# Joint transposes of q and k, an earlier x of pair 1, and four idle products in a fused attention and spectral-mix kernel

## The chip, the cores and the metric

The kernel runs on one core of one Trainium2 chip. A core has TensorE (matrix products into PSUM), VectorE, ScalarE and GpSimd, a queue engine (SyncE, called SP in the profile) and 16 DMA engines. The metric is the device time of one execution in microseconds (us); the median of several executions is compared.

## The reference

What is computed, cut to what matters:

```python
def _attn_ref(q, k, v, s):                       # q, k, v: (8, 8, 576, 64); s: (8, 8, 576)
    scores = np.matmul(q, k.transpose(0, 1, 3, 2)) / np.sqrt(64)
    cum = np.cumsum(np.maximum(s, 0.0), axis=-1)
    bias = -(cum[:, :, :, None] - cum[:, :, None, :])
    scores = np.where(causal, -1e9, scores + np.minimum(bias, 0.0))
    return np.matmul(softmax(scores), v)

def _moe_ref(x, w_r, w_i, w_ch):                 # x: (8, 576, 512); w_r, w_i: (64, 512, 512)
    X = np.fft.rfft(x, axis=1)                   # only the first 64 modes are mixed
    Yr = einsum('bmd,mde->bme', Xr, w_r) - einsum('bmd,mde->bme', Xi, w_i)
    Yi = einsum('bmd,mde->bme', Xr, w_i) + einsum('bmd,mde->bme', Xi, w_r)
    u = x + np.fft.irfft(Y, n=576, axis=1)
    return u + np.maximum(u @ w_ch, 0.0)
```

The heads of the attention's output, laid side by side, are the x of the second part.

## The kernel before

**Attention.** The loop over `n` (line 564) runs 32 times; each turn, called a sequence here, does two heads of one batch entry: group `g` of four (two heads each, 128 columns of x), batch entry `b`. A q/k tile (`loads_qk`, line 148) holds two sequences: q of both heads stands in partitions 0 to 63 and k in 64 to 127, each partition with 18 rows of 64 values. `transposes` (line 332) turns it into `qt` and `kt`, which have the 64 head values in the partitions: 36 products of 64x64 on TensorE in two halves of 18, q into PSUM partitions 0 to 63 and k into 64 to 127 of the tile `tr_ps`, which has one buffer; then four copies out of PSUM: q and k of the first half and q of the second on VectorE, k of the second on ScalarE (line 344). The transposes of sequence n + 1 are made in turn n, the halves around `scores(n, 1)`. `scores` (line 366) makes score products and their exponentials on ScalarE (line 390), `av` (line 401) the product with v and the division by the sum (VectorE, `den`, `rcp`, `x_all`), `fft` (line 435) the forward transform of x into `xs`.

**Modes.** For each group the 64 modes are mixed in eight chunks of eight modes (`modes`, line 455): 16 products of 32 columns with weights that stream in from DRAM, summed over the groups in `y_acc`. Chunks of the first three groups are put among the sequences (`mode_steps`, line 239); those of the last group come after attention. A chunk has four quarters of weights: real and imaginary, and for each four of its eight modes. All weight, q, k and v loads are issued by GpSimd's queue in the order of the program (line 234), each once the place that it fills is free.

**x times w_ch.** The output is cut into 18 pairs of 128-token tiles. For a pair, `x_transposed` (line 629) transposes x and VectorE casts it out of PSUM, and `x_times_wch` (line 644) multiplies it with w_ch. Pairs 0 and 1 keep this product open in PSUM until y is known; pair 1 consists of half tiles. In the last sequences (`first_pairs`, line 512) and among the last group's chunks (`work`, line 718) other pairs' products are made ahead.

**The end.** After the last group's chunks 0 to 5 (line 833) follow chunk six (line 852) and chunk seven (line 868). `y_transposed` transposes a chunk's result and ScalarE copies it, `y_times_wch` multiplies it with w_ch and VectorE casts that to `v_sb`, which SP spreads into `yv` (`spread`, line 496); `gather` (line 688) does this in bulk for earlier chunks. In chunk seven the products of pairs 0 and 1 that need no last chunk (`first_u`, `first_z`) are put ahead of the third and the last quarter. `auxpool` has two PSUM buffers that `yp`, `yt_ps`, `v_ps` and others take in turn. The string of steps at line 924 finishes all pairs.

Each engine runs its instructions in program order, so where a step is written decides what it stands behind.

Of the kernel before, what the change touches and what calls it, by code (L numbers as in the profile page):

```python
# [9 lines left out]
FP32 = mybir.dt.float32  # L10
FP16 = mybir.dt.float16
BF16 = mybir.dt.bfloat16
# [6 lines left out]
def kernel(  # L19
# [11 lines left out]
    nc = tc.nc  # L31
    B, H, S, D = q.shape
    NM = moe_w_r.shape[0]
    DM = H * D
# [16 lines left out]
    NF = NT - 1  # L51
    RP = P // 4
    R = S // RP
    RH = R // 2
    W = 2 * P
    NWN = S // W
    NK = 2 * NWN
# [271 lines left out]
        for h in range(2):  # L329
            nc.sync.dma_start(out=qt[n % NQ][D : D + 1, h, :], in_=ncum_sb[p0 + h : p0 + h + 1, :])  # L330

    def transposes(n, half):
        if n >= N:
            return
        src = loaded[n][:, n % 2, :].rearrange("p (r d) -> p r d", d=D)[:, half * RH : half * RH + RH]
        ps = trpool.tile([P, RH, 2 * RP], BF16, name="tr_ps", tag="tr")
        for r in range(RH):
            for i in range(2):
                rows = slice(HP * i, HP * i + HP)
                nc.tensor.transpose(ps[rows, r, :], src[rows, r, :], ident16[rows, rows])  # L340
        for i, dst in enumerate((qt, kt)):
            copy = (nc.vector.tensor_copy, nc.scalar.copy)[half * i]
            to = dst[n % NQ][:D].rearrange("d h (p r) -> d h p r", r=R)
            copy(  # L344
                out=to[:, :, :, half * RH : half * RH + RH],
                in_=ps[HP * i : HP * i + HP].rearrange("d r (h p) -> d h p r", h=2),
            )

    def scores4(n, ps):
# [51 lines left out]
    def av(n, h):  # L401
        if n < 0:
            return
        g, b = divmod(n, B)
        pt = p_sb[(2 * n + h) % NP_]
        ps = avpool.tile([P, NT, VW], FP32, name="av_ps", tag="av")
        todo = []
        for I in range(NT):
            t0 = first_token(b, I)
            for x in range(2 * min((t0 + P - 1) // W + 1, NWN)):  # L410
                w, r = divmod(x, 2)
                o = poff[x] + t0 - w * W
                todo.append((I, r, pt[:, o : o + P], v2[n % NV][:, bass.ds((2 * w + h) * W + P - 1 + NCH * r, NCH)]))
        rows = slice(NL * h, NL * h + NL)
        todo.append((NT - 1 - b % 2, 1, p4[n % 2][rows, :], v4[g % 2][rows, b, :NCH]))

        for i, (I, r, lhsT, rhs) in enumerate(todo):
            nc.tensor.matmul(  # L418
                ps[:, I, r : r + NCH], lhsT, rhs, start=(i == 0), stop=(i == len(todo) - 1),
                skip_group_check=True,  # L420
            )
        den = rpool.tile([P, NT], FP32, name="den", tag="den")
        nc.vector.tensor_reduce(  # L423
            out=den, in_=ps[:, :, 0 : VW : NCH], axis=mybir.AxisListType.X, op=ALU.add
        )
        rcp = rpool.tile([P, NT], FP32, name="rcp", tag="rcp")
        nc.vector.reciprocal(out=rcp, in_=den)
        nc.vector.tensor_tensor(  # L428
            out=x_all[:, g, b, :, D * h : D * h + D],
            in0=ps[:, :, 1 : NCH],  # L430
            in1=rcp.unsqueeze(2).to_broadcast([P, NT, D]),
            op=ALU.mult,
        )

    def fft(n):
        if n < 0:
            return
        g, b = divmod(n, B)
        ps = auxpool.tile([P, 2, 3 * HM], FP32, name="ft_ps", tag="aux")
        for T in range(NT):  # L440
            nT = tails[T]
            for q_ in range(2):
                nc.tensor.matmul(  # L443
                    ps[HP * q_ : HP * q_ + HP].rearrange("p h f -> p (h f)"),
                    x_all[:nT, g, b, T, q_::2], Ff_sb[:nT, T, :],
                    start=(T == 0), stop=(T == NT - 1),
                    tile_position=(0, HP * q_), skip_group_check=True,
                )
        for h in range(2):
            for q_ in range(2):  # L450
                a = ps[HP * q_ : HP * q_ + HP, h, : 2 * HM].rearrange("p (r m) -> p r m", r=2)
                a = bass.AP(tensor=a.tensor, offset=a.offset, ap=[a.ap[0], [HM, 2]] + list(a.ap[1:]))
                nc.vector.tensor_copy(out=xs[g % 2][HP * h : HP * h + HP, q_, :, h, :, b, :], in_=a)  # L453
# [102 lines left out]
    with tc.tile_pool(name="sc_psum", bufs=2, space=PSUM) as scpool, \  # L556
            tc.tile_pool(name="tr_psum", bufs=1, space=PSUM) as trpool, \
            tc.tile_pool(name="av_psum", bufs=1, space=PSUM) as avpool:
        cum_rows(0)
        transposes(0, 0)  # L560
        transposes(0, 1)
        load(loads_qk(2) + loads_v(2))
        pad_p()
        for n in range(N):
            if n in (0, 2):
                nc.vector.memset(xs_flat[n // 2].bitcast(FP32), 0.0)
            tails_due = loads_tails(n // B + 1)[n % B - 3 : n % B - 2] if 2 < n % B < 5 else []
            load((loads_qk(n + LA) if n % 2 else []) + loads_v(n + LA) + tails_due, loads_w(on_chip[n]))
            cum_rows(n + 1)
            scores(n, 0)  # L570
            av(n - 1, 1)
            if n % B:
                mode_products(n)
            transposes(n + 1, 0)
            scores(n, 1)
            i = first_pairs[n - N + len(first_pairs)] if n >= N - len(first_pairs) else None
            if i is not None:
                first_transposed(i, 0)
            transposes(n + 1, 1)
            fft(n - 1)  # L580
            av(n, 0)
            if i is not None:
                first_product(i, 0)
                first_transposed(i, 1)
            if n % B == 0:
                mode_products(n)
            if i is not None:
                first_product(i, 1)
            if n == N // 2:
                nc.gpsimd.dma_start(out=wch_sb, in_=moe_w_ch.rearrange("(dt p) e -> p dt e", p=P))  # L590
        av(N - 1, 1)
        fft(N - 1)
# [36 lines left out]
    def x_transposed(i):  # L629
        xts[i] = xt_sb[len(xts) % 2]  # L630
        for x, (b, T) in enumerate(pairs[i]):
            ps = upool.tile([P, DT, P], FP32, name="xt_ps", tag="u")
            for rows, bb, ident in parts(b, T):
                for dt in range(DT):
                    nc.tensor.matmul(
                        ps[:, dt, rows], x_all[: rows.stop - rows.start, dt, bb, T, :],
                        ident, start=True, stop=True, skip_group_check=True,
                    )
            nc.vector.tensor_copy(out=xts[i][:, x], in_=ps)  # L639
# [4 lines left out]
    def x_times_wch(i, last):  # L644
        for x in range(2):
            start_z(i, x)
            for dt in range(DT):
                nc.tensor.matmul(  # L648
                    zs[i, x], xts[i][:, x, dt, :], wch_sb[:, dt, :],
                    start=(dt == 0), stop=(last and dt == DT - 1), skip_group_check=True,  # L650
                )
# [25 lines left out]
    def y_times_wch(c, yt):  # L677
        vp = auxpool.tile([P, DM], FP32, name="v_ps", tag="aux")
        for dt in range(DT):
            nc.tensor.matmul(  # L680
                vp, yt[:, dt, :], wch_sb[:, dt, :], start=(dt == 0), stop=(dt == DT - 1)
            )
        vb = spool.tile([P, DM], FP16, name="v_sb", tag="v")
        nc.vector.tensor_copy(out=vb, in_=vp)
        spread(c, 1, vb)
        return vb
# [146 lines left out]
    for c in range(NCK - 2):  # L833
        yb = modes(NG - 1, c)
        for x in range(TAKE[c] - 1):
            work()
        if c == NCK - 3:
            x_transposed(0)
        yt = y_transposed(yb, c)
        if TAKE[c]:  # L840
            work()
        if c >= NY:
            if c == NCK - 3:
                x_times_wch(0, False)
            y_times_wch(c, yt)
            if c == NCK - 3:
                gather(NY, NCK - 2, (), (0,))
        elif c == NY - 1:
            gather(0, NY, (1, 3), (1, 0))
    assert not order_z and not ahead  # L850
    c = NCK - 2
    yb6 = modes(NG - 1, c)
    x_transposed(1)
    yt = y_transposed(yb6)
    x_times_wch(1, False)
    vb6 = y_times_wch(c, yt)


    def first_u():
        add_x(0)  # L860
        add_y(u_of(0), 0, 0, slice(0, GK))
        add_last(u_of(0), 0, yb6, c=0)

    def first_z(i):
        add_y(z_of(i), i, 1, slice(0, GK))
        add_last(z_of(i), i, vb6, c=0)

    yb = modes(NG - 1, NCK - 1, {2: lambda: (first_u(), first_z(0)), 3: lambda: first_z(1)})

    yt = spool.tile([P, DT, P], FP16, name="yt_sb", tag="yt")  # L870
    for x in range(2):
# [95 lines left out]
```

The softmax here doesn't subtract the row's maximum and nothing guards it: scores larger than these inputs give would overflow.

## Time and profile before

| What | Value |
|---|---|
| median of 6 runs | 444.13 us (443.84 to 445.58) |
| profiled execution, its own time | 445.08 us |
| its span, first to last instruction | 443.0 us |
| mean granted TensorE clock | 0.923 |
| TensorE busy | 341.1 us (77%) |
| VectorE busy | 253.0 us (57%) |
| ScalarE busy | 226.1 us (51%) |
| GpSimd busy | 246.1 us (56%) |
| moved by DMA | 93.25 MB, mean 210 GB/s |
| chain that ended last | DMA 61%, PE 18%, DVE 9% of the span |

How to read it: the page cuts the span into 40 equal slices and gives each engine's busy share in each; "PEclk" is the TensorE clock that was granted, in tenths of full speed. "The chain of waits" follows the last instruction back, at each step to what released it; a line has its start, its length in us, its engine, tile and kernel line, and the number of instructions. In the timeline a line has the start, the busy time, the engine, the kernel line, the operation, what is written from what, and the shape; in brackets the idle time before it and what ended it. In a table of stretches, a row has the stretch, its length, and for TensorE, its weight loads, VectorE, ScalarE and GpSimd the busy time and the number of instructions; then the granted clock, the DMA share and GB/s. Engines: PE is TensorE, DVE VectorE, ACT ScalarE, POOL GpSimd. An engine's idle time costs nothing unless something on the path to the end waits for it.

### The profile page before, as it was taken

The numbers are of one execution on the slowest core, as the hardware profiler recorded it, in microseconds if no ns is written. First come the engines' busy times: TensorE is split into PE (matmuls) and PEld (weight loads), VectorE is DVE, ScalarE is ACT, GpSimd is POOL, SyncE is SP. The second block draws the span as 40 slices with busy tenths as digits, with TensorE's granted clock in tenths as the row PEclk, the third lists the DMA queues.
The fourth block names the chain that finished last, engine by engine and source line by source line (L and its number), as shares of the span: only waits on it lengthen the run. The fifth ranks groups of instructions, "written<-read, shape, count | busy, mean of one in ns | idle before, by whom it ended". The sixth has DMA issues, their size and how long they took to land.

```text
span 443.0 us, 10830 instructions
## 1 busy us (share of the span) xinstructions
PE 341.1 (77%) x4411; PEld 206.6 (47%) x4411; DVE 253.0 (57%) x574; ACT 226.1 (51%) x421; POOL 246.1 (56%) x385
## 2 busy tenths in 40 slices
PE   0788988988676996593946928898987987749994
PEld 0455655655454653361634505555653445324441
DVE  7766776666545664462633605767655454432696
ACT  1476787367544643472543604665650544320794
POOL 7765665565565656365655546465644444440495
PEclk9998999999969798988895968999997999988998
DMA  9999999999999999999999999999999999997498
GB/s 175 201 206 206 204 206 205 207 206 206 209 194 205 205 208 206 209 206 208 204 206 205 209 208 198 206 205 206 192 208 211 209 210 210 210 217 155 145 388 344
DMA packets 72768, 93.25 MB, mean 210 GB/s; under 512 B 29760, under 2 KB 31296, under 8 KB 72720
## 3 DMA queue, kind: packets, MB, share of 16 engines
q0 software_dynamic: 63408, 81.29, 104.8%
q1 hardware_dynamic: 9312, 11.29, 7.6%
q8 instruction: 34, 0.56, 0.5%
q14 instruction: 14, 0.11, 0.1%
HBM read 163.51 MB, written 9.44 MB: 390 GB/s over the span
## 4 chain that ended last, share of the span: by engine, by line
DMA 61%; PE 18%; DVE 9%; issue 4%; POOL 4%; ACT 3%; POOLq 0%; SPq 0%; DVEq 0%
DMA w_sb<-in_moe_w_i_dram 35%; DMA w_sb<-in_moe_w_r_dram 17%; DMA qk<-in_k_dram 6%; PE sc_ps L382 3%; PE yp L463 3%; DMA qk<-in_q_dram 2%; DVE qt L344 2%; POOL w_sb L234 2%; PE sc_ps L376 2%; PE tr_ps L340 2%; PE av_ps L418 2%; DVE kt L344 1%; DMA xs<-c_negm 1%; DVE xs L453 1%; DVE x_all L428 1%
## 5 line engine op out<-in xcount | busy, mean ns | idle before, releaser
L390 ACT ACTIVATE p_sb<-sc_ps,cumt_sb 128x576 f16<-128x576 f32 (+1 forms) x256 | 141.6, 635 | 33.7 <-PE sc_ps L382 33.3
L234 POOL DMA_DIRECT2D w_sb<-in_moe_w_r_dram x120 | 71.2, 595 | 58.4 <-DMA w_sb<-in_moe_w_r_dram 18.3
L234 POOL DMA_DIRECT2D w_sb<-in_moe_w_i_dram x120 | 71.0, 593 | 52.0 <-DMA w_sb<-in_moe_w_i_dram 19.5
L382 PE MATMUL sc_ps<-qt,kt 128*128 128x512 bf16 (+2 forms) x384 | 77.2, 313 | 4.5 <-ACT kt L344 3.8
L344 DVE COPY qt<-tr_ps 64x576 bf16<-64x576 bf16 x64 | 47.8, 747 | 56.0 <-PE tr_ps L340 56.0
L234 POOL DMA_DIRECT2D v<-in_v_dram x72 | 52.0, 722 | 41.1 <-DMA w_sb<-in_moe_w_r_dram 10.0
L340 PE MATMUL tr_ps<-ident,qk 64*64 64x64 bf16 x1152 | 34.9, 205 | 40.4 <-DMA qk<-in_k_dram 16.5
L463 PE MATMUL yp<-w_sb,xs 128*32 128x512 bf16 (+1 forms) x480 | 43.2, 413 | 24.9 <-DMA w_sb<-in_moe_w_i_dram 18.0
L361 ACT ACTIVATE p<-sc_ps,cumt 128x64 f16<-128x64 f32 x32 | 10.0, 313 | 89.5 <-PE sc_ps L357 89.5
L376 PE MATMUL sc_ps<-negm,ident 128*128 128x256 bf16 x256 | 53.8, 295 | 0.0
L382 PEld LDWEIGHTS <-kt 128*128 128x128 bf16 x384 | 38.7, 105 | 31.8 <-ACT kt L344 9.5
L340 PEld LDWEIGHTS <-qk 64*64 64x64 bf16 x1152 | 26.5, 117 | 56.5 <-DMA qk<-in_k_dram 17.4
L418 PE MATMUL av_ps<-v,p_sb 128*128 128x65 f16 x1024 | 43.7, 196 | 1.2 <-DVE x_all L428 0.5
L418 PEld LDWEIGHTS <-p_sb 128*128 128x128 f16 x1024 | 37.3, 99 | 8.3 <-DVE x_all L428 3.4
L463 PEld LDWEIGHTS <-xs 128*32 128x32 bf16 (+1 forms) x512 | 19.2, 144 | 42.5 <-DMA w_sb<-in_moe_w_i_dram 17.4
L453 DVE CAST xs<-ft_ps 64x128 bf16<-64x128 f32 x128 | 36.6, 286 | 3.2 <-PE ft_ps L443 1.8
L423 DVE TENSOR_REDUCE den<-av_ps 128x5 f32<-128x10 f32 x64 | 10.8, 169 | 41.7 <-PE av_ps L418 40.7
L428 DVE TENSOR_TENSOR x_all<-av_ps,rcp 128x320 f16<-128x320 f32 x64 | 31.5, 492 | 2.2
L344 ACT COPY kt<-tr_ps 64x576 bf16<-64x576 bf16 x32 | 22.9, 715 | 15.5 <-DVE qt L344 14.9
L443 PE MATMUL ft_ps<-Ff_sb,x_all 128*64 128x192 f16 (+1 forms) x320 | 24.5, 267 | 1.0 <-DVE x_all L428 1.0
L648 PE MATMUL z_ps<-wch_sb,xs 128*128 128x512 f16 x96 | 24.6, 402 | 0.2 <-DVE xs L639 0.2
L344 DVE COPY kt<-tr_ps 64x576 bf16<-64x576 bf16 x32 | 24.4, 763 | 0.4
(113 smaller groups left out, 422.7 us busy)
## 6 DMA issues: line engine op xcount, KB each, us to landing
w_sb<-in_moe_w_r_dram POOLq DMA_DIRECT2D x120, 256.0 KB, 8.5
w_sb<-in_moe_w_i_dram POOLq DMA_DIRECT2D x117, 256.0 KB, 8.9
out_dram<-r_w SPq DMA_DIRECT2D x16, 512.0 KB, 2.8
v<-in_v_dram POOLq DMA_DIRECT2D x72, 64.0 KB, 7.4
qk<-in_q_dram POOLq DMA_DIRECT2D x15, 288.0 KB, 8.4
qk<-in_k_dram POOLq DMA_DIRECT2D x15, 288.0 KB, 9.0
x_all<-in_moe_w_i_dram POOLq DMA_DIRECT2D x6, 256.0 KB, 7.6
y_acc<-in_moe_w_r_dram POOLq DMA_DIRECT2D x4, 256.0 KB, 7.2
```

The source lines that it names most:

```text
L234: nc.gpsimd.dma_start(out=dst, in_=src)
L340: nc.tensor.transpose(ps[rows, r, :], src[rows, r, :], ident16[rows, rows])
L344: copy(out=to[:, :, :, half * RH : half * RH + RH], in_=ps[HP * i : HP * i + HP].rearrange("d r (h p) -> d h p r", h=2),)
L376: nc.tensor.matmul(ps[:, bass.ds(w * S, W)], ident16, negm[:, bass.ts(r, W)], start=True, stop=False, skip_group_check=True,)
L382: nc.tensor.matmul(ps[:, c0 : c0 + i1 - i0], keys[:, w, r, :], qh[:, i0:i1], start=False, stop=True, skip_group_check=True,)
L390: nc.scalar.activation(out=pt[:, poff[x] : poff[x] + S - w * W], in_=ps[:, w * S : (w + 1) * S - w * W], func=ACTF.Exp, bias=cumt_sb[:, x, ...
L418: nc.tensor.matmul(ps[:, I, r : r + NCH], lhsT, rhs, start=(i == 0), stop=(i == len(todo) - 1), skip_group_check=True,)
L428: nc.vector.tensor_tensor(out=x_all[:, g, b, :, D * h : D * h + D], in0=ps[:, :, 1 : NCH], in1=rcp.unsqueeze(2).to_broadcast([P, NT, D]), ...
L443: nc.tensor.matmul(ps[HP * q_ : HP * q_ + HP].rearrange("p h f -> p (h f)"), x_all[:nT, g, b, T, q_::2], Ff_sb[:nT, T, :], start=(T == 0), ...
L453: nc.vector.tensor_copy(out=xs[g % 2][HP * h : HP * h + HP, q_, :, h, :, b, :], in_=a)
L463: nc.tensor.matmul(ps[32 * cg : 32 * cg + 32, :], cols[k0:, q_, 1 - ri, :, c * MC // 2 + cg], wt[(g, c, ri, cg // 2)][k0:, 2 * (cg % 2) + ...
L648: nc.tensor.matmul(zs[i, x], xts[i][:, x, dt, :], wch_sb[:, dt, :], start=(dt == 0), stop=(last and dt == DT - 1), skip_group_check=True,)
```

## The change

It has three parts.

1. `transposes` works in thirds. One product transposes q and k of six rows each at a time over all 128 partitions, so that q and k of both heads stand side by side in 128 columns of the same 64 PSUM partitions. A sequence has 18 products instead of 36 and six copies instead of four: q of every third and k of the first on VectorE, k of the second and the third on ScalarE. The last third is written behind `fft(n - 1)` and ahead of `av(n, 0)`.
2. `x_transposed(1)` and `x_times_wch(1, False)` are made with chunk five, the second behind `gather`, instead of with chunk six.
3. Just ahead of chunk seven's last quarter stand four products of 128x512 into a PSUM tile of `auxpool` that nothing reads.

```diff
-    RH = R // 2
+    RH = R // 3
...
-    def transposes(n, half):
+    def transposes(n, third):
         if n >= N:
             return
-        src = loaded[n][:, n % 2, :].rearrange("p (r d) -> p r d", d=D)[:, half * RH : half * RH + RH]
-        ps = trpool.tile([P, RH, 2 * RP], BF16, name="tr_ps", tag="tr")
+        part = slice(third * RH, third * RH + RH)
+        src = loaded[n][:, n % 2, :].rearrange("p (r d) -> p r d", d=D)[:, part]
+        ps = trpool.tile([HP, RH, P], BF16, name="tr_ps", tag="tr")
         for r in range(RH):
-            for i in range(2):
-                rows = slice(HP * i, HP * i + HP)
-                nc.tensor.transpose(ps[rows, r, :], src[rows, r, :], ident16[rows, rows])
+            nc.tensor.transpose(ps[:, r, :], src[:, r, :], ident16)
         for i, dst in enumerate((qt, kt)):
-            copy = (nc.vector.tensor_copy, nc.scalar.copy)[half * i]
+            copy = nc.scalar.copy if i and third else nc.vector.tensor_copy
             to = dst[n % NQ][:D].rearrange("d h (p r) -> d h p r", r=R)
             copy(
-                out=to[:, :, :, half * RH : half * RH + RH],
-                in_=ps[HP * i : HP * i + HP].rearrange("d r (h p) -> d h p r", h=2),
+                out=to[:, :, :, part],
+                in_=ps[:, :, HP * i : HP * i + HP].rearrange("d r (h p) -> d h p r", h=2),
             )
...
-        transposes(0, 0)
-        transposes(0, 1)
+        for third in range(3):
+            transposes(0, third)
...
             transposes(n + 1, 1)
             fft(n - 1)
+            transposes(n + 1, 2)
             av(n, 0)
...
             if c == NCK - 3:
                 x_times_wch(0, False)
+                x_transposed(1)
             y_times_wch(c, yt)
             if c == NCK - 3:
                 gather(NY, NCK - 2, (), (0,))
+                x_times_wch(1, False)
...
     yb6 = modes(NG - 1, c)
-    x_transposed(1)
     yt = y_transposed(yb6)
-    x_times_wch(1, False)
     vb6 = y_times_wch(c, yt)
...
+    idle_ps = auxpool.tile([P, DM], FP32, name="idle_ps", tag="aux")
+
+    def idle_products(n):
+
+        for i in range(n):
+            nc.tensor.matmul(idle_ps, ident16h, wch_sb[:, 0, :], start=True, stop=True, skip_group_check=True)
+
-    yb = modes(NG - 1, NCK - 1, {2: lambda: (first_u(), first_z(0)), 3: lambda: first_z(1)})
+    yb = modes(NG - 1, NCK - 1, {2: lambda: (first_u(), first_z(0)), 3: lambda: (first_z(1), idle_products(4))})
```

## The prediction

> **What bounds the kernel now.** I read the page first, then the chain of waits, then the waits of GpSimd's queue, then the timeline of one attention sequence and of the last 60 us.
>
> ```profile
> span 443.0 us, 10830 instructions
> PEclk9998999999969798988895968999997999988998
> DMA  9999999999999999999999999999999999997498
> GB/s 175 201 206 206 204 206 205 207 206 206 209 194 205 205 208 206 209 206 208 204 206 205 209 208 198 206 205 206 192 208 211 209 210 210 210 217 155 145 388 344
> ```
>
> The DMA engines are full in every slice up to about 405 us, at some 206 GB/s whatever the engines compute. So up to there the 64 MB of weights set the pace, and attention matters only where it frees a weight, v or q/k buffer too late or reaches the last weights too late. GpSimd issues those loads; its rows near 390 us stand 0.4 and 0.9 us apart, each let go by an older load's landing. In slices 36 and 37 the DMA runs empty and the last stage begins. The chain there:
>
> ```profile
> 398.13 1.07 PE yp L463 x3
> 399.20 0.96 PE xt_ps L635 x16
> 400.16 0.54 PE yt_ps L672 x4
> 400.70 2.64 PE z_ps L648 x8
> 403.34 0.86 PE v_ps L680 x4
> 404.20 0.59 PE yp L463 x8
> ...
> 407.07 0.58 PE yp L463 x4
> 407.65 0.55 PE z_ps L744 x4
> 408.20 0.43 PE z_ps L755 x4
> 408.64 0.60 PE yp L463 x4
> ```
>
> From 398.13, where chunk six's last weights land, to the end of the last quarter at 409.24 TensorE never pauses. It looks like the bound, but the landings are close behind. The rows of the last four loads: issued at 393.14 and 395.20 (third quarter, 11.0 and 11.1 us to landing) and at 396.76 and 398.37 (last quarter, 10.6 and 9.9 us). So the third quarter's weights are there at 406.3 and the last quarter's at 408.3; TensorE opened those quarters at 407.0 and 408.56. **At most 0.2 us can be won at the last quarter** unless weights land earlier. From 409.24 to 443.0 no line is changed, and I carry those 33.8 us over.
>
> **Part one, the transposes.** Per sequence, before: 36 products of 64x64 in two groups of 0.47 us; four copies of 576 columns, three on VectorE (0.75, 0.76, 0.75) and one on ScalarE (0.715). After: 18 products of 128 columns in three groups. Four 128x128 transposes take 0.39 (0.22 + 3 x 0.057), so six take 0.22 + 5 x 0.057 = 0.50. A copy has 384 columns: VectorE takes 0.69 for 512 and 0.43 for 256, so 0.56; ScalarE 0.58 and 0.35, so 0.47, or 0.54 if its 576-column row is scaled with a small fixed part; I take 0.50. VectorE: 4 x 0.56 = 2.24 against 2.26. ScalarE: 1.00 against 0.72. As work that is nothing. The **order** costs:
>
> ```profile
> 308.30 2.20 ACT L390 ACTIVATE p_sb<-sc_ps,cumt_sb 128x576 f16<-128x576 f32 x4
> 309.00 0.47 PE L340 MATMUL tr_ps<-ident,qk 64*64 64x64 bf16 x18
> 309.59 0.74 DVE L344 COPY qt<-tr_ps 64x576 bf16<-64x576 bf16 x1
> 310.05 0.67 PE L418 MATMUL av_ps<-v,p_sb 128*128 128x65 f16 x16
> 310.52 0.72 ACT L344 COPY kt<-tr_ps 64x576 bf16<-64x576 bf16 x1
> 312.31 0.68 DVE L538 CAST xt<-xt_ps 128x512 f16<-128x512 f32 x1
> 313.05 1.04 PE L546 MATMUL z_ps<-wch_sb,xt 128*128 128x512 f16 x4 [1.00 <-DVE xt L538]
> ```
>
> tr_ps has one buffer. The new third group stands on TensorE behind the FFT and ahead of av, and must wait until ScalarE has copied k of the second group, which it does only after four exponentials: 310.52 + 0.50 = 311.03. So the third group starts at 311.05, av at 311.4 instead of 310.05. Behind it wait the division (311.47 becomes 312.25), the product at 310.78 (becomes 312.1), the next x transposes and their cast (312.31 becomes 313.4), and the product at 313.05, which becomes 314.1: **1.05 us a sequence**. The five sequences 27 to 31 have no weight wait of TensorE among them after 275.6, so attention ends 5 x 1.05 = 5.3 us later (bounds: 4.0 if the shorter first copies win 0.25 each time, 6 if ScalarE's copies take 0.54 and more). Earlier sequences lose up to 1.4 each, because their scores wait for the last k copy too, but TensorE waits there for q and k (14.9 and 16.5 us) and for weights (18.0 and 3.4), and the loss ends in those waits.
>
> The Trainium skill, page "PSUM — Partial Sum Buffer", section "PSUM bank collisions raise a hardware error", speaks against this layout: two engines may not touch one bank in the same 32 partitions at once, and the two halves now share partitions 0 to 63 where they had 0 to 63 and 64 to 127. The row says that nothing was overlapped anyway: ScalarE's k copy waited for VectorE's q copy, 14.9 us in 7 times. With or without the rule the sum for the late sequences is the same.
>
> Who is hurt by 5.3 us? Of the loads, q of the third pair of sequences goes out at 23.21 against a last transpose at 21.2; it slips by about 0.9, with six or more loads still in flight. The first load into chunk 28's places goes out at 385.21, its products having ended at 382.0: 3.2 us of margin, just enough. Of the compute, TensorE waits 1.87 us for weights at 355.95, which leaves 3.4; then it stands idle 1.88 and 2.73 us before chunk six (393.92 and 398.13).
>
> **Part two, x of pair 1.** It moves 16 + 8 products and two casts (1.28 us of VectorE) ahead of chunk six; it issues no DMA. The transposes go ahead of the v product, so the casts stand ahead of VectorE's v_sb cast, and behind that SP's spread of chunk five: some 0.7 us later, not read before 404.8. The eight products (1.9) run where TensorE waits for the gather's copies, so chunk six starts about 0.7 later, 394.6, needs 1.1, and its last weights come at 398.12: room for 2.4 us of the 3.4 that are left. On the path 0.96 + 2.64 = 3.60 go away, but they were a cover: v_ps now waits for ScalarE's copy (0.58), and idle_ps takes the PSUM buffer that yp of the last chunk had, so yp takes v_ps's and waits for VectorE's cast (0.69). At half clock: 398.13 + 1.07 + 0.80 (y_sb) + 0.55 + 0.65 + 1.65 + 0.75 = 403.6, then 0.6 and ten products (404.80 to 407.07, 2.27): third quarter at 406.45. At full clock 405.1. Both are met by the landing at 406.3; at full clock another 1.2 us of lateness is covered, so 1.0 us left over from part one just fits.
>
> **Part three, the idle products.** Four of 128x512 cost what the v product costs, 0.86. Third quarter to last quarter was 407.00 to 408.56, 1.56. So the last quarter opens at 406.34 + 1.56 + 0.86 = 408.76: 0.42 after its weights (408.34) and 0.20 after the old 408.56. Bounds: -0.21 if the third quarter is early enough to hide them, +0.42 if the old kernel was already held by the landing.
>
> The clock, as the rows have it:
>
> ```profile
> 392.10:395.50 3.40, 1.09 (x10) 0.48 (x10) 2.08 (x4) 1.72 (x3) 1.25 (x3) 1.00 1.11 208
> 395.50:398.90 3.40, 0.77 (x6) 0.21 (x6) 0.42 (x1) 0.00 (x0) 1.42 (x3) 0.50 1.13 223
> 398.90:402.30 3.40, 3.40 (x27) 1.83 (x26) 1.89 (x3) 0.58 (x1) 0.06 (x1) 0.50 1.12 210
> ```
>
> A stretch with 1.09 us of TensorE work (second number) was followed by half clock (0.50). The moved products fill it. "TensorE: Matmul & The Clock Gate", Part 1, has the clock fall after an idle window of about 3.4 us; here it fell after one that was a third busy. By that rule the idle products would protect nothing, since a wait of 0.4 us is no window; by the row they might. The sum holds either way.
>
> **The sum.** Profiled execution: 445.08, which is 443.0 of span and 2.08 around it; +0.20 gives 445.28. The median, 444.13, is 0.95 shorter, so I suppose its last quarter was held by the landing alone, and take +0.42: 444.55, rounded up to **444.6**.
>
> **Rivals.**
> Attention's lateness comes through (slower). Place: the third group behind ScalarE's copy. It decides from 5.5 us at the end of attention on, for 1.87 + 2.4 + 1.2 = 5.5 are covered. With 6 us, and one more half-clock stretch of the kind after 337 us (chunk 24's products took 3.07 against 1.09, 2.0 more), 8.0 - 5.5 + 0.42 = 2.9, or 447.0; with half of it 445.6. For it: it uses up every cover I found. Against: the median runs may have more cover than the profiled one.
> The weights land earlier and TensorE was the bound (faster). Then the last quarter opens at 405.1 + 1.56 + 0.86 = 407.5 instead of 408.56, -1.1, 443.0. For it: half clock until 402.3 on the path. Against: landings at 406.3 and 408.3.
> The change does nothing that shows: idle products hidden, landing holds, -0.2, 443.9.
>
> **Numbers.** Forecast 0.38 (444.1 to 445.0 by itself), lateness 0.36, early weights 0.20, nothing 0.06. A measurement here tells some 0.2% (0.9 us) from no change. Faster: 0.18 + 0.01 = 0.19. Same: 0.33 + 0.01 + 0.02 + 0.05 = 0.41. Slower: 0.05 + 0.35 = 0.40. The range takes in early weights just below 443.0 and lateness to 447.0.
>
> **What would show it.** A wait of TensorE before the third group for ScalarE's k copy, about 1 us in late sequences; attention ending 4 to 6 us later at unchanged GB/s; TensorE idle before the third quarter, none before the last, which opens after the idle products; everything from there on 34 us. I am wrong if the last weights land at another time, or if TensorE still has no wait for weights from 356 to 406.

## The result, and the profile after

The changed kernel takes 447.49 us (median of 16 runs, 445.53 to 451.68) against 444.30 us of the kernel before (35 runs) on the same chip: a ratio of 1.0073, 95% interval 1.0058 to 1.0089. That is slower, by 3.2 us there. On two other chips (runs e10 and e17 below) the same kernel was 1.8 and 2.0 us slower. The forecast of 444.6 us was wrong, and 447.49 lies just above its range, which ends at 447.0. The execution that was profiled took 449.12 us, 1.6 us more than the median; that of the kernel before took 445.08.

The page of the changed kernel, the same rows as before:

```profile
span 447.3 us, 9770 instructions
...
PEclk9989999999989999798988969999997798998998
DMA  9999999999999999999999999999999999992597
GB/s 180 202 204 206 203 206 205 206 209 206 207 202 207 206 207 204 207 207 208 205 207 206 208 202 205 206 207 205 209 211 208 210 210 209 207 217 50 197 386 287
```

The weights stream at the same 206 GB/s. What differs is the end: the last slice moves 287 GB/s instead of 344.

One late sequence, in the timeline (start, busy time, engine, line; in brackets the idle time before and its releaser):

```profile
312.28 1.17 ACT L389 ACTIVATE p_sb<-sc_ps,cumt_sb 128x576 f16<-128x576 f32 x2
312.54 0.54 DVE L343 COPY qt<-tr_ps 64x384 bf16<-64x384 bf16 x1
313.31 0.48 ACT L343 COPY kt<-tr_ps 64x384 bf16<-64x384 bf16 x1
313.84 0.49 PE L339 MATMUL tr_ps<-ident,qk 128*64 128x128 bf16 x6 [0.97 <-ACT kt L343]
314.27 0.67 PE L417 MATMUL av_ps<-v,p_sb 128*128 128x65 f16 x16
```

The third group waits 0.97 us for ScalarE's copy of k, which stands behind the exponentials, and av waits behind it. Attention's last av begins at 338.4 us instead of 333.3. The waits of TensorE over the whole run tell what became of the 5.1 us. A row has the total, the number of times and the longest; the first row is of the kernel before, the others of the changed one:

```profile
PE yp L463 <- DMA w_sb<-in_moe_w_i_dram: 18.0, 11, 3.3
...
PE tr_ps L339 <- ACT kt L343: 34.2, 32, 1.7
...
PE yp L462 <- DMA w_sb<-in_moe_w_i_dram: 5.5, 2, 3.3
```

None of the waits for weights that are left lies behind 265 us: TensorE no longer waits for the weights of the last group. The chain of waits at the end:

```profile
400.24 0.59 ACT yv L711
400.82 0.02 issue
400.85 0.71 DVE yv L709
401.55 0.02 issue
401.57 0.70 DVE y_sb L486
...
403.39 1.89 PE v_ps L680 x4
405.28 1.02 PE yp L462 x8
...
410.18 0.97 PE idle_ps L873 x4
411.15 0.60 PE yp L462 x4
```

There is no transfer in it from 396 us on. Chunk six's y_sb stands on VectorE behind the gather's copies, the products behind it run at half clock, and the four idle products stand on the path with all their 0.97 us. The last quarter opens at 411.08 instead of 408.57.

Its weights had landed at 406.05 us already. That is 2.5 of the 4.3 us by which the two profiled spans differ. The other 1.8 us come after the last addition, where the last writes take longer. The row of the kernel before, then that of the changed one:

```profile
out_dram<-r_w SPq DMA_DIRECT2D x16, 512.0 KB, 2.8
...
out_dram<-r_w SPq DMA_DIRECT2D x16, 512.0 KB, 4.7
```

The last number is the median time from issue to landing, for the same 16 writes of the same size.

### The profile page after: what moved, and what is told of

Same layout as the page of the kernel before. It is cut to its first block, busy times and chain, and to the rows that moved or that the text cites. A ratio compares the mean times of both kernels' runs of the same rounds, so it can differ in the third digit from the quotient of the medians.

```text
span 447.3 us, 9770 instructions
## 1 busy us (share of the span) xinstructions
PE 349.0 (78%) x3839; PEld 218.2 (49%) x3839; DVE 249.4 (56%) x606; ACT 230.2 (51%) x453; POOL 246.3 (55%) x385
## 4 chain that ended last, share of the span: by engine, by line
PE 40%; DMA 32%; ACT 12%; DVE 9%; issue 3%; POOL 2%; SPq 0%; POOLq 0%; DVEq 0%; ACTq 0%
DMA w_sb<-in_moe_w_r_dram 19%; DMA w_sb<-in_moe_w_i_dram 12%; ACT p_sb L389 7%; PE yp L462 6%; PE sc_ps L381 5%; PE z_ps L648 5%; PE tr_ps L339 4%; PE av_ps L417 4%; PE sc_ps L375 3%; PE z_ps L545 2%; ACT kt L343 2%; DVE qt L343 1%; PE g_ps L699 1%; PE xt_ps L635 1%; POOL w_sb L234 1%
## 5 line engine op out<-in xcount | busy, mean ns | idle before, releaser
L339 PE MATMUL tr_ps<-ident,qk 128*64 128x128 bf16 x576 | 53.0, 232 | 51.8 <-ACT kt L343 34.2
L343 DVE COPY qt<-tr_ps 64x384 bf16<-64x384 bf16 x96 | 52.4, 546 | 58.4 <-PE tr_ps L339 58.1
L381 PE MATMUL sc_ps<-qt,kt 128*128 128x512 bf16 (+2 forms) x384 | 75.3, 308 | 3.7 <-ACT kt L343 1.9
L339 PEld LDWEIGHTS <-qk 128*64 128x64 bf16 x576 | 39.9, 116 | 66.6 <-issue 45.3
L343 ACT COPY kt<-tr_ps 64x384 bf16<-64x384 bf16 x64 | 30.7, 479 | 51.4 <-DVE qt L343 51.1
L381 PEld LDWEIGHTS <-kt 128*128 128x128 bf16 x384 | 37.8, 103 | 31.4 <-ACT kt L343 10.3
L462 PE MATMUL yp<-w_sb,xs 128*32 128x512 bf16 (+1 forms) x480 | 40.3, 412 | 9.1 <-DMA w_sb<-in_moe_w_i_dram 5.5
L417 PEld LDWEIGHTS <-p_sb 128*128 128x128 f16 x1024 | 38.4, 99 | 4.5 <-issue 0.2
L442 PE MATMUL ft_ps<-Ff_sb,x_all 128*64 128x192 f16 (+1 forms) x320 | 28.1, 259 | 1.0 <-DVE x_all L427 1.0
L375 PEld LDWEIGHTS <-ident 128*128 128x128 bf16 x256 | 18.0, 99 | 9.9 <-issue 2.2
```

Of the source, the lines that this page charges most:

```text
L339: nc.tensor.transpose(ps[:, r, :], src[:, r, :], ident16)
L343: copy(out=to[:, :, :, part], in_=ps[:, :, HP * i : HP * i + HP].rearrange("d r (h p) -> d h p r", h=2),)
L375: nc.tensor.matmul(ps[:, bass.ds(w * S, W)], ident16, negm[:, bass.ts(r, W)], start=True, stop=False, skip_group_check=True,)
L381: nc.tensor.matmul(ps[:, c0 : c0 + i1 - i0], keys[:, w, r, :], qh[:, i0:i1], start=False, stop=True, skip_group_check=True,)
L417: nc.tensor.matmul(ps[:, I, r : r + NCH], lhsT, rhs, start=(i == 0), stop=(i == len(todo) - 1), skip_group_check=True,)
L442: nc.tensor.matmul(ps[HP * q_ : HP * q_ + HP].rearrange("p h f -> p (h f)"), x_all[:nT, g, b, T, q_::2], Ff_sb[:nT, T, :], start=(T == 0), ...
```

## How the runs are read

Every run's profile gives six numbers, in us. "av" is the start of attention's last av, from the timeline; "half" is the time at half clock from there to the last quarter, from the records of the granted clock; "landed" is when the last load of chunk seven's weights has landed, from its issue and its time to landing; "last quarter" is the start of chunk seven's last four yp products; "tail" is the span's end less that; "fetch" is how far behind the last quarter the last packet of an instruction queue of 16 KB begins, from the DMA records. All profiles but one take 30.85 to 31.11 us from the last quarter to the end of the last addition (e4 takes 32.02, since TensorE waits 1.08 us for yv there), so the tail differs by the last writes.

| Run | time | ratio, 95% interval | av | half | landed | last quarter | tail | fetch |
|---|---|---|---|---|---|---|---|---|
| before | | | 333.3 | 13.7 | 408.30 | 408.57 | 34.43 | 3.4 |
| changed | 447.49 | 1.0073, 1.0058-1.0089 | 338.4 | 17.1 | 406.05 | 411.08 | 36.24 | 12.9 |
| e1 part one | 448.79 | 1.0100, 1.0087-1.0113 | 340.7 | 13.7 | 408.64 | 410.75 | 35.58 | 13.5 |
| e2 part two | 444.30 | 0.9999, 0.9989-1.0009 | 332.8 | 13.7 | 407.24 | 407.59 | 34.43 | 3.4 |
| e3 part three | 445.61 | 1.0026, 1.0012-1.0041 | 333.7 | 10.2 | 407.16 | 408.28 | 34.69 | 2.6 |
| e4 two and three | 445.05 | 1.0022, 1.0006-1.0038 | 332.9 | 17.1 | 407.47 | 408.44 | 35.59 | 2.7 |
| e5 thirds early | 445.16 | 1.0020, 1.0007-1.0032 | 333.3 | 10.2 | 407.16 | 407.20 | 36.54 | 22.0 |
| e6 thirds last five | 447.73 | 1.0069, 1.0050-1.0088 | 340.2 | 13.7 | 406.06 | 410.86 | 36.08 | 21.8 |
| e7 behind av | 449.02 | 1.0099, 1.0082-1.0116 | 340.4 | 17.1 | 409.52 | 412.07 | 35.92 | 14.7 |
| e8 one and two | 445.17 | 1.0027, 1.0011-1.0044 | 338.6 | 10.2 | 406.74 | 407.87 | 35.57 | 13.5 |
| e9 delay alone | 446.48 | 1.0050, 1.0038-1.0063 | 337.6 | 6.8 | 407.74 | 407.79 | 36.29 | 19.9 |
| e10 changed | 446.22 | 1.0040, 1.0024-1.0057 | 340.2 | 10.2 | 406.39 | 409.89 | 35.13 | 11.8 |
| e11 one and two | 445.15 | 1.0025, 1.0009-1.0040 | 338.4 | 3.4 | 406.72 | 406.76 | 35.78 | 13.2 |
| e12 waits filled | 444.18 | 0.9998, 0.9985-1.0012 | 340.4 | 3.4 | 407.23 | 408.62 | 34.59 | 8.6 |
| e13 fetch moved | 446.12 | 1.0040, 1.0026-1.0053 | 333.5 | 20.5 | 407.73 | 407.77 | 36.51 | 20.0 |
| e14 changed, fetch moved | 446.57 | 1.0046, 1.0029-1.0062 | 338.9 | 13.7 | 406.70 | 410.39 | 34.66 | 2.5 |
| e15 clock and fetch | 443.79 | 0.9990, 0.9980-1.0001 | 339.0 | 0 | 407.37 | 407.41 | 34.60 | 3.2 |
| e16 delay, fetch moved | 445.03 | 1.0018, 1.0001-1.0036 | 337.5 | 13.7 | 407.41 | 408.15 | 34.43 | 3.7 |
| e17 changed | 446.39 | 1.0039, 1.0024-1.0054 | 338.4 | 10.2 | 407.13 | 409.06 | 36.17 | 11.9 |
| e18 changed, fetch moved | 445.52 | 1.0018, 1.0001-1.0036 | 338.6 | 10.2 | 407.41 | 408.43 | 34.60 | 2.7 |

Runs e1 to e4, e5 to e8, e9 to e12, e13 to e16 and e17 to e18 were measured together, each set on one chip; the kernel before had medians of 444.44, 444.28, 444.38, 444.64 and 444.40 us there. The last two sets have the same chip number on record. A profile is one execution; its last quarter moves by a microsecond or more from one execution of a kernel to the next (409.06 to 411.08 for the changed kernel). The difference of landed and last quarter says what held it: 0.04 us where TensorE waited for the weights, more where TensorE itself came late.

The time of an execution is longer than its span, by 2.06 to 2.12 us (medians) in the kernels with halves and by 1.74 to 1.81 us in those with thirds in all or the first 27 sequences (e6 has 1.89). So inside the span the changed kernel loses 0.3 us more than its time says; what makes this difference is not shown.

## Experiments one: which part

Theory A was that attention's lateness comes through, theory B that the loss is made at the end by the other two parts.

**e1, part one alone** (the body of `transposes` as in the change).

```diff
-        transposes(0, 0)
-        transposes(0, 1)
+        for third in range(3):
+            transposes(0, third)
...
             fft(n - 1)
+            transposes(n + 1, 2)
             av(n, 0)
```

> The kernel before with part one alone (transposes in thirds). Theory A, lateness: attention ends 5.2 us later, that is more than the waits behind it cover, so TensorE and not the landing of the last weights opens the last quarter; without the idle products (0.97 us measured in the changed kernel) the time is 446.0 to 446.8. Theory B, the end: the 5.2 us are covered and the loss comes from the other two parts; 444.0 to 444.8. Under A the profile has no wait for weights on TensorE from about 356 us to chunk seven's last quarter; under B it has one of 0.3 us or more ahead of that quarter.

Measured: 448.79, a loss of 4.35 us and so more than the whole change. Against e2's profile, of the same chip and with part two in place of part one, 3.16 us are at the last quarter and 1.15 in the tail. The chain shows what lateness does where x of pair 1 still stands behind chunk six:

```profile
400.29 0.70 DVE y_sb L486
400.99 0.05 issue
401.04 0.61 PE yt_ps L672 x4
401.65 3.58 PE z_ps L648 x8
405.23 1.16 PE v_ps L680 x4
```

The eight z products take 3.58 us here, 2.64 before: the half-clock stretch, 398.9 to 405.7, lies wholly behind the start of chunk six instead of partly over its wait for weights. This run's weights also landed late, at 408.64, and the last quarter opened 2.1 us behind them.

**e2, part two alone.**

```diff
             if c == NCK - 3:
                 x_times_wch(0, False)
+                x_transposed(1)
...
                 gather(NY, NCK - 2, (), (0,))
+                x_times_wch(1, False)
```

> The kernel before with part two alone (x of pair 1 ahead of chunk six). Theory A, lateness from part one: 443.9 to 444.5, because the last weights still land at about 408.3 us and hold the last quarter. Theory B, the end: if the copies behind which chunk six's y_sb now stands are the loss, 445.0 to 446.0. If instead the kernel before was bound by TensorE there, 443.2 to 443.8.

Measured: 444.30, no difference. The last quarter opened at 407.59 without a wait for weights, 0.35 us behind their landing, so TensorE held it in this execution, but only just.

**e3, part three alone.**

```diff
+    idle_ps = auxpool.tile([P, DM], FP32, name="idle_ps", tag="aux")
...
-    yb = modes(NG - 1, NCK - 1, {2: lambda: (first_u(), first_z(0)), 3: lambda: first_z(1)})
+    yb = modes(NG - 1, NCK - 1, {2: lambda: (first_u(), first_z(0)), 3: lambda: (first_z(1), idle_products(4))})
```

> The kernel before with part three alone (four idle products ahead of the last quarter). Theory A: they fill a part of the wait for the last weights and the rest shows, +0.3 to +0.6, 444.6 to 444.9. Theory B: TensorE was the bound already, so all 0.9 to 1.0 us shows, 445.2 to 445.4. If the landing hides them, 444.1 to 444.4.

Measured: 445.61, +1.17 us, a little above theory B's range. Theory A's reading of the landing fails here: the weights had landed at 407.16, and the chain has the products in full, with no transfer between:

```profile
406.95 0.43 PE z_ps L755 x4
407.38 0.97 PE idle_ps L873 x4
408.35 0.60 PE yp L463 x4
```

**e4, the change without part one** (e2 and e3 together).

> The changed kernel without part one (transposes in halves as before; x of pair 1 early; idle products). Theory A, lateness: the loss is nearly gone, 444.2 to 444.9. Theory B, the end: most of the loss of 3.2 us stays, 446 to 447.5.

Measured: 445.05, just above theory A's bound. Most of the loss is gone without the thirds, as theory A has it. Against e2 the idle products cost 0.75 us here, against 1.17 in e3.

## Experiments two: which sequences, and the order

**e5 and e6, thirds for a part of the sequences.** `in_halves` is the function before; e6 has the condition the other way round.

```diff
     def transposes(n, third):
         if n >= N:
             return
+        if n > 26:
+            return in_halves(n, third) if third < 2 else None
```

> Part one alone, but sequences 27 to 31 are transposed in halves as before; the thirds stay for sequences 0 to 26. Theory A, lateness of the last five sequences: the waits for q, k and weights before 275 us swallow the rest, so the time is that of before, 444.0 to 445.0. Rival C, the thirds cost wherever they stand (more copies, an earlier load that goes out late): most of part one's +4.35 us stays, 447 to 449.

> The other way round: thirds for sequences 27 to 31 alone, halves before. Theory A: all of part one's loss, 448 to 449.3, attention's last product about 5 us later than before. Rival C: 444.5 to 446.

Measured: e5 445.16, a little above A's bound, though its attention ends at 333.3 as before and its last quarter, at 407.20, waits for weights; its 0.88 us are in the tail of 36.54. e6: 447.73, a little below A's range. So the late sequences make most of the loss, and something else, in the tail, is there wherever the thirds are.

**e7, the third group behind av**, in part one alone.

```diff
             fft(n - 1)
-            transposes(n + 1, 2)
             av(n, 0)
+            transposes(n + 1, 2)
```

> Part one alone, but the third group of transposes is written behind av instead of ahead of it, so that TensorE's wait of 0.96 us for ScalarE's copy is filled by av's products and the division isn't delayed; the number of products and copies is that of part one. Theory A: a late sequence loses 0 to 0.4 us instead of 1.0, attention ends 0 to 2 us late, 444.2 to 446. Rival C, the copies and products cost, not their order: 447.5 to 449.

Measured: 449.02, against theory A. Two av in a late sequence are 10.5 us apart (321.8 to 332.4), between the 10.2 of before and the 11.3 of e1, so the wait did shrink as expected. But the last av came at 340.4 all the same: GpSimd's timeline has a weight load held by the products of a chunk for 7.5 us (4.3 at most in the other profiles), and a half-clock stretch fell at 308 us.

```profile
98.10 0.59 POOL L234 DMA_DIRECT2D w_sb<-in_moe_w_r_dram  x1 [7.54 <-PE yp L462]
```

Why the order brings that is open, and this run doesn't tell A from C.

**e8, the change without the idle products** (e1 and e2 together).

> The changed kernel without the idle products. Theory A with the products on TensorE's path: 0.9 to 1.1 us less than the changed kernel, 446.3 to 446.8; against part one alone (448.79) that gives part two about -2.2 us, because it takes x of pair 1 off a path that has become TensorE's. Rival D, the idle products keep the clock up and so pay for themselves: 447.3 or more. If part two gives nothing, 448.5 to 449.

Measured: 445.17, below every theory's range. Attention ends at 338.6, 5.3 us late, and yet the last quarter opens at 407.87, earlier than in the profile of before. So with part two most of the lateness is covered; the last quarter still opens 1.1 us behind its weights. Part two, worth nothing alone, is worth 3.6 us between the medians (two chips) where part one is in, 2.9 of them at the last quarter of the profiles (410.75 to 407.87).

## Experiments three: delay, idle products, clock

**e9, the delay alone**, in the kernel before.

```diff
+        if h == 0 and N - 7 < n < N - 1:
+            for i in range(8):
+                nc.tensor.matmul(
+                    ps.rearrange("p t c -> p (t c)"), ident16h, wch_sb[:, 0, : NT * VW], start=True, stop=True,
...
         for i, (I, r, lhsT, rhs) in enumerate(todo):
```

> The kernel before (transposes in halves) with eight products of 128x330 that nothing reads ahead of av in each of the last five such sequences, about 1.1 us each by the 0.22 us that a product of 512 columns takes: attention's end is delayed by some 5.5 us with no other change. Theory A, lateness of attention's end is the whole cause of part one's loss: as the thirds in the last five sequences alone (447.73), 447.0 to 448.5. Rival C, the thirds' copies cost: 444.2 to 445.2, since nothing of theirs is here. If only the half clock matters, which a busy TensorE doesn't get, 444.5 to 446.

Measured: 446.48, between the theories. The profile says why: the last quarter opened at 407.79 after a wait of 0.68 us for its weights, so 4 us of delay were covered, and the loss is in a tail of 36.29. The DMA's view of 426.5 to 429.5 us, in the midst of the output's writes, has:

```profile
q1 hardware_dynamic: 572, 1.11, 95.5%
q8 instruction: 1, 0.02, 3.5%
issues: line engine op xcount, KB each, median us to landing
out_dram<-r_w SPq DMA_DIRECT2D x3, 512.0 KB, 4.8
```

One packet of instructions, 16 KB. The kernel before has its last such packet at 411.9, when no output is being written yet; its first output write goes out at 414.1.

**e10 and e11, the changed kernel with and without the idle products on one chip.**

> The changed kernel once more, on the chip of the next run, to price the idle products. If their 0.97 us on TensorE's path is their whole price, it stands 0.9 to 1.1 us above the next; if they cost 2 us and more, as the comparison over two chips has it (447.49 against 445.17), something behind the last quarter loses too.

> The changed kernel without the idle products, again: 444.9 to 445.5, and 0.9 to 1.1 us below the run before it if their own time is their whole price.

Measured: 446.22 and 445.15, a difference of 1.07 us between the medians, with intervals that overlap: their own time is about their price. e11's last quarter waited 0.56 us for weights and opened at 406.76.

**e12, the changed kernel with TensorE's waits at the end of attention filled.**

```diff
+        if n == N - 1:
+            flat = ps.rearrange("p h f -> p (h f)")
+            for i in range(10):
+                nc.tensor.matmul(
+                    flat, ident16h, wch_sb[:, 0, : flat.shape[-1]], start=True, stop=True, skip_group_check=True
...
+        for i in range({0: 4, NCK - 2: 0}.get(c, 0) if g == NG - 1 else 0):
+            nc.tensor.matmul(ps, ident16h, wch_sb[:, 0, :], start=True, stop=True, skip_group_check=True)
```

> The changed kernel with 14 more products that nothing reads in TensorE's waits at the end of attention (ten of 192 columns ahead of the last FFT, four of 512 ahead of chunk 24; 1.0 and 0.98 us of waits stood there). Theory E, the half-clock stretches there (10.2 us of them in the changed kernel's profile) make the lateness come through: the granted clock stays 1.00 from 335 to 352 us, TensorE is 3 us and more earlier at chunk 25, and the time falls to 445.0 to 446.4. If the clock falls all the same, or if the lateness is regained in later waits anyway, 447 to 448.

Measured: 444.18, below the expected range, 2.04 us below e10 and level with the kernel before. Stretches of e10 (second number TensorE's busy time; third from the end the granted clock):

```profile
336.80:340.20 3.40, 2.48 (x23) 1.28 (x20) 2.34 (x8) 1.15 (x3) 1.08 (x2) 1.00 1.11 205
340.20:343.60 3.40, 1.53 (x28) 1.04 (x26) 1.65 (x6) 0.58 (x1) 1.77 (x3) 1.00 1.13 210
343.60:347.00 3.40, 3.28 (x16) 0.84 (x16) 1.12 (x4) 0.00 (x0) 1.46 (x3) 0.51 1.12 209
347.00:350.40 3.40, 2.94 (x22) 2.04 (x20) 3.15 (x5) 0.00 (x0) 1.49 (x3) 0.50 1.14 214
```

and of e12:

```profile
338.30:341.70 3.40, 2.48 (x34) 1.74 (x32) 1.54 (x6) 1.17 (x2) 1.57 (x3) 1.00 1.14 212
341.70:345.10 3.40, 3.30 (x31) 1.45 (x28) 2.32 (x7) 0.00 (x0) 0.95 (x3) 1.00 1.11 207
345.10:348.50 3.40, 2.33 (x24) 1.36 (x22) 2.33 (x4) 0.00 (x0) 2.20 (x4) 1.00 1.12 210
```

In e10 a stretch with 1.53 us of work was followed by half clock; in e12, with the waits filled, the least is 2.33 and the clock stays. The busy time alone doesn't decide it: in e17 a stretch with 2.41 us (340.8 to 344.2) was followed by half clock, and in e15 one with 1.85 us (395.4 to 398.8) was not. TensorE reaches chunk 25 at 352.55 instead of 354.20 and the last quarter 1.27 us earlier. But this run isn't pure: its 28 more TensorE instructions also brought the fetch from 11.8 to 8.6 us and the tail from 35.13 to 34.59. So at most 1.3 of the profiles' 1.8 us belong to the clock, and the changed kernel's own profiles differ there by 2.0 us; what carries weight is the 2.04 us between the medians, for clock and fetch together.

## Experiments four: the fetch

Theory F: the last instruction fetch costs time if it falls among the output's writes, and it moves with the number of TensorE's instructions; the thirds have 18 products and their weight loads for 36.

**e13, the kernel before with 40 small products**, and **e16, e9 with 84**.

```diff
         ps = auxpool.tile([P, 2, 3 * HM], FP32, name="ft_ps", tag="aux")
+        flat = ps.rearrange("p h f -> p (h f)")
+        for i in range(4 if 8 <= n < 18 else 0):
+            nc.tensor.matmul(flat[:, :8], ident16h, Ff_sb[:, 0, :8], start=True, stop=True, skip_group_check=True)
```

> The kernel before with 40 products of 8 columns that nothing reads, four in each of sequences 8 to 17, where TensorE waits for weights anyway; they are 80 more TensorE instructions and bring the last instruction fetch to some 20 us behind the last quarter, into the output's writes. Theory F, the fetch: last quarter as before, but the last write 1.2 to 1.9 us later, 445.6 to 446.4. Theory A, lateness alone: nothing of it here, 444.1 to 444.7.

> The kernel with the delay alone (e9, 446.48) and 84 small products in sequences 6 to 17 (168 instructions), which bring its last fetch from 19.9 to about 3 us behind the last quarter. Theory F: the delay of 5 us is covered and the fetch was the loss, 444.3 to 445.0. Theory A: the delay was the loss, 446.2 to 446.8.

Measured: e13 446.12 against 444.64 of before, +1.48 us, with the fetch at 20.0 us, the last quarter at 407.77 and a tail of 36.51. The last quarter opened as its weights landed and earlier than in the profile of before, so in this execution the loss is all behind it, where no line differs. The DMA's view of 427 to 430 us has the packet:

```profile
q1 hardware_dynamic: 569, 1.10, 95.5%
q8 instruction: 1, 0.02, 3.7%
```

e16: 445.03, at theory F's upper bound, so e9's ratio of 1.0050 falls to 1.0018 (e9's and e16's chips differ) when the fetch goes back to 3.7 us. Four microseconds of delay cost 0.4 us between the medians, 0.8 by the ratio (0.04 to 1.6). e16's writes, over the whole run:

```profile
out_dram<-r_w SPq DMA_DIRECT2D x16, 512.0 KB, 2.8
```

and the end of e9, 440.9 to 442.9 us, in steps of 0.05 us:

```profile
GB/s 41 0 41 41 0 41 41 0 41 0 41 41 0 41 0 41 41 0 41 41 0 41 0 41 41 0 41 41 0 41 0 41 41 0 0 0 0 0 0 0
```

After all other traffic has ended, single packets of 2 KB follow each other for 1.6 us. e13 has the same string at its end; e16 and the kernel before have none.

**e14, the changed kernel with 55 small products** (sequences 8 to 18, five each), and **e17 and e18, the changed kernel and e14's once more on one chip.**

> The changed kernel with 55 such small products in sequences 8 to 18 (110 instructions), which bring its last fetch from 12.9 to about 3 us behind the last quarter. Theory F: the span ends 34.4 to 34.5 us behind the last quarter's opening instead of 35.1 to 36.2, and the time falls by 0.7 to 1.8 us against the changed kernel (446.22 and 447.49 on two chips), to 445.0 to 446.0. Theory A: 446.2 to 447.5 as it was.

> The changed kernel, on one chip with the next run. 446.2 to 447.5, as on the two chips before.

> The changed kernel with the 55 small products, as in e14. Theory F: 0.7 to 1.8 us below the run before it. If the changed kernel's loss is all TensorE's lateness ahead of the last quarter, the same within 0.4 us.

Measured: e14 had the tail that F expects, 34.66, but its time of 446.57 missed: its last quarter opened at 410.39, 3.7 us behind its weights, after 13.7 us at half clock. Measured together, e17 took 446.39 and e18 445.52: 0.87 us, within F's range. But the two intervals against the kernel before overlap, and e14 and e18 are the same kernel with medians 1.05 us apart. So in the changed kernel the fetch's cost is seen in the tails (35.13 to 36.24 us against 34.60 and 34.66), and its size in the time isn't clear of noise.

**e15, parts one and two, the waits filled as in e12, and the fetch moved.**

> Parts one and two without the idle products, with the 14 products in the waits at the end of attention (as in e12) and 40 small ones in sequences 8 to 17 (108 instructions in all). If the clock and the fetch are the causes, the last quarter opens at 406 to 407 us and the span ends 34.4 us later: 442.5 to 443.6, faster than both kernels. If lateness still comes through, 444 to 446.

Measured: 443.79, just above the expected range, against 444.64, a ratio of 0.9990 (0.9980 to 1.0001). The clock was never halved from 269 to 439 us, and the last quarter waited for its weights:

```profile
PEclk9999989999999999988895968999999999999998
...
407.41 0.65 PE L471 MATMUL yp<-w_sb,xs 128*32 128x512 bf16 x4 [0.99 <-DMA w_sb<-in_moe_w_i_dram]
```

So in this execution the late attention costs nothing at the last quarter: what is left is the landing. It is ahead of both kernels by its median, by less than a measurement tells from no change.

## Why the prediction was wrong

**What bounds the kernel.** Up to 405 us the weights' stream set the pace, as said. The step that failed is the next one: "At most 0.2 us can be won at the last quarter", since its weights are there at 408.3, and on it the sum that opens the last quarter of the changed kernel 0.42 us behind that landing. The reading of the rows was right, but it was one execution. With attention on time the last weights landed at 407.16 to 407.73 in the other profiles (e2 to e5, e13), and in the changed kernel's three profiles at 406.05, 406.39 and 407.13; its last quarter opened 5.0, 3.5 and 1.9 us behind them, of which the idle products are 0.97. So TensorE was the bound and not the landing. Both signs that the prediction named for being wrong came: the weights landed at another time, and in the first profile TensorE had no wait for weights from 356 to 406 us.

**Part one.** The order's cost was right: a wait of 0.97 us (about 1.0 forecast), copies of 0.546 and 0.479 us (0.56 and 0.50), 0.49 for six transposes (0.50), attention's end 5.1 us late (5.3). That nothing overlapped before was read from a row of 14.9 us in 7 times, 12.8 of which are one wait; in the trace no k copy of ScalarE begins ahead of the q copy's end in any of the 32 sequences, so the conclusion stands. The step "1.87 + 2.4 + 1.2 = 5.5 are covered" failed as a sum of three named waits. How much is covered depends on part two (e1 against e8) and goes with the half clock behind attention. e16 delays attention alone by 4 us and loses 0.4 at the median; e11 has 5.1 us and a last quarter that waits for weights; in the changed kernel's three profiles 1.0 to 4.1 us were left at the last quarter behind the landing.

**Part two.** It was forecast as the loss of a cover and the gain of 3.60 us of path. Alone it showed neither (e2); with a late attention it gave 2.9 us at the last quarter. The forecast path has no wait of chunk six's y_sb behind the gather's copies on VectorE; in the first profile it ended at 402.27 instead of 400.0 and the third quarter opened at 408.54 instead of 406.45.

**Part three.** This term was mis-sized: forecast at 0.42 us, its upper bound, because the landing was to hide the rest. The runs showed 1.07 (e10 against e11), 1.17 (e3) and 0.75 (e4 against e2), and the products take 0.97 in the chains.

**The tail.** The step "no line is changed, and I carry those 33.8 us over" failed. The compute is the same to 0.02 us, but 572 fewer products with their weight loads (by the page's counts) moved an instruction fetch into the output's writes: the tail grew by 0.7 to 1.8 us in the three profiles. In the time this cost 1.48 us in e13; between the medians of e17 and e18 it is 0.87. The 2.08 us around the span were carried over too, and are 1.78 in the changed kernel.

**The sum.** On two chips the changed kernel lost 1.84 and 1.99 us, 2.15 and 2.30 inside the span. Idle products and fetch make 1.07 + 0.87 = 1.94, which leaves 0.2 to 0.4 us for the lateness at the median; each term is a difference of two medians with intervals that overlap, so this gives sizes and proves no split. On the first chip it lost 3.19, and why there 1.2 us more is open. Its profile has the longest half clock, but over all executions the mean granted clock has the same median there (0.943) as in e10 (0.943) and e17 (0.945). Within the first chip's 16 executions a low clock does go with a long time: the seven below 0.942 have a median of 449.06 us, the nine above 447.37.

**The rivals.** The number fell beside "Attention's lateness comes through"; its mechanism holds in full without part two (e1, e6), and with it in the executions with much half clock. "The weights land earlier" was true of the landing and wrong in its sign, since the idle products, the lateness and the tail took more than it gave.

## What to carry to other kernels

Before a landing in one profile is used as a bound, compare it with the landings of other executions; here it was about a microsecond later than in most, and work put behind it cost its full time. A delay is cheap where waits follow, but here half clock followed such waits and made the work behind them longer; filling the waits removed one such stretch, and with the moved fetch that was worth 2 us (e12). An edit that changes the number of instructions moves the fetches of instructions: look where the last ones lie against saturated transfers, even if the code there is unchanged.

## What the runs showed of the hardware

**Instruction fetches in the DMA.** Each profile has 30 to 35 packets of 16 KB in an instruction queue during the run, each 0.9 to 1.9 us long, with 240 to 263 of TensorE's recorded instructions (medians) from one to the next. In the profiles with the last one 2.5 to 3.7 us behind the last quarter the tail is 34.43 to 34.69 us (e4's wait apart); 8.6 us behind, 34.59; and 11.8 to 22 us behind, 35.13 to 36.54. The Trainium skill, page "Runtime: NRT & Kernel Launch", section "Instruction fetch mechanics", has an engine's instruction memory refilled in blocks of 16 KiB, 256 instructions, while it runs, which agrees; but it calls the cost of crossing a block's boundary mostly hidden, and here one block among saturated writes cost 1.48 us (e13).

**The clock.** Half-clock stretches last 3.4, 6.8, 10.2 or 13.7 us, and partly lie elsewhere in each execution of one kernel (10.2 to 17.1 us of them between attention's end and the last quarter in the changed kernel's three profiles). The skill's page "TensorE: Matmul & The Clock Gate", Part 1, says that the window is free-running, which agrees; but it has the clock fall after an idle window, and in e10 a stretch with 1.53 us of work in 3.4 was enough.
